# Attention with two expert layers: two state-read buffers, rank sums on TensorE, routing steps side by side

## The chip, the cores and the metric

The kernel runs on one core of one Trainium2 chip. The metric is the time on the device in microseconds, as the median of several runs; lower is better. In the rows PE is TensorE and PEld its weight loads, DVE is VectorE, ACT is ScalarE, POOL is GpSimd, and SP is SyncE, which issues most DMAs.

## What is computed

An attention in both directions between 512 tokens and 32 state slots gives four batches of 544 rows, N = 2176 rows of 512 columns. Two expert layers follow; the first has a capacity per expert, so a row's rank among the rows of its expert matters. The reference, cut:

```python
a  = softmax(scale * x @ state.T);  xread = a  @ state    # x (4, 8, 512, 64), state (4, 8, 32, 64)
a2 = softmax(scale * state @ x.T);  sread = a2 @ x
x  = concat([xread, sread], axis=2).transpose(0, 2, 1, 3).reshape(N, 512)
# layer 1: 8 experts, w1 (8, 512, 1024), w2 (8, 1024, 512); layer 2 the same, without cap
logits = x @ w_gate; expert = argmax(logits); gate = softmax(logits)[expert]
for i in range(N):
    e = expert[i]
    if counts[e] < cap: disp[e, counts[e]] = x[i]; pos[i] = counts[e]; counts[e] += 1; keep[i] = True
y = relu(disp @ w1) @ w2
out[i] = gate[i] * y[expert[i], pos[i]] if keep[i] else 0
```

## The kernel before

**Attention.** `slot(b)` works on batch b: it transposes the softmax of the state side (`e2n`), reads the state for the tokens (`av`) and the tokens for the state (`sr`), and makes scores and softmax of later batches beside it. A slot has seven places, `beside(0)` to `beside(6)`, at which side work runs. The three steps of `sread(b)` stand at places 3, 5 and 6, and those of batches 2 and 3 run on into the next slot or behind the last: `fold` adds the heads on TensorE into a bank `pyT` of PSUM, lets ScalarE copy it to `xs`, and writes `xs` to rows of `xrows` in DRAM; `turn` transposes `xs`; `logits` multiplies it by the gate's weights. The rows of the tokens go to `xrows` from `av`.

**Background work.** Small steps of the routing are generators in one queue, `bgq`. `tick(n)` takes up to n steps of it, `PAUSE` ends a turn, and `abreast` takes steps of several generators in turn. So the order of each engine's instructions is fixed when the program is built, by where `tick` is called: at the places of a slot (99 steps each, from the second slot on) and after each four matmuls (m1) or three (m2) of an expert's product, TQ steps a time. Such a point is called an event.

**Routing.** `route(b0, nb, stops)` handles nb batches: the one-hot of the argmax, the number of earlier rows for the same expert, then `places` (rank, position in the lists) and `gates`, abreast; `stops` are pauses between these parts. It is called for batch 0 alone (`early`), from whose counts `popular` and `load_first` choose and load the first expert's weights, and for batches 1 to 3 in the first expert's product. For the count a VectorE chain adds the rows of a partition (`csb`), two matmuls (`upper`, `ones`) add over the partitions, and VectorE adds batch by batch into `preb`. `plan_runs` then chooses which expert's block runs when; `enlist_all` makes for each batch two one-hots, `loc` and `lov`, and multiplies them on TensorE (list products, five small matmuls a batch) to have lists of rows.

**Expert products.** TensorE runs blocks in the order m1(0), m1(1), m2(0), m1(2), m2(1), ... An m1 block is 12 matmuls into a bank `ph`, an m2 block 12 into four banks `py`. In fp32 each weight and each activation is split in a high part, rounded by a copy to fp32r, and a low part, a subtraction: `xTh`/`xTl`, `hTh`/`hTl`, `w0h`/`w0l` for w1 and `w1h`/`w1l` for w2. ScalarE rounds; VectorE or GpSimd subtracts. `SPLIT0` gives the slot and place at which the four parts of the first w1 are split, `SPLIT2` the events for w2. At the event `PLANNED` the kernel waits (in program order) until the plan is made and asks for the next expert's weights. `fills` writes zeros into `yrows`, the output rows of the first layer, and `fill_out` into `out`, both through SyncE's queue.

Of the kernel before, what the change touches and what calls it, by code (L numbers as in the profile page):

```python
# [74 lines left out]
def moe_kernel(ctx: ExitStack, tc: tile.TileContext, x, state, wg1, w1a, w2a, cap, wg2, w1b, w2b, out):  # L75
# [87 lines left out]
    DVE.memset(wg2q, 0.0)  # L163
    zb = ctile([P, 4 * P], BF16, "zb")
    DVE.memset(zb, 0.0)
# [8 lines left out]
    sums = [ctile([P, P], F32, f"sums{i}") for i in range(2)]  # L174

    zeros = tp.tile([P, ROW], F32, name="zeros")

# [20 lines left out]
    upper = ctile([P, P], BF16, "upper")  # L198
    ones = ctile([P, P], BF16, "ones")
    tidc = ctile([P, B, R + 1], F32, "tidc")  # L200
    tidw = ctile([P, B, R + 1], F32, "tidw")
    smask = ctile([P, B, R + 1], F32, "smask")

    def constants():
        DVE.tensor_scalar(upper, iof[:, 0:P], iop[:, 0:1], None, op0=ALU.is_gt)

        DVE.tensor_scalar(tidc, tid, float(HALF), None, op0=ALU.is_ge)
# [11 lines left out]
        POOL.memset(zeros, 0.0)  # L219
# [53 lines left out]

    def wsplit(which, c, on=ON[2]):
# [376 lines left out]

    def route(b0, nb, stops, early=False):
# [3 lines left out]
        o4, cs, p4 = ohb[:, b0:b0 + nb], csb[:, b0:b0 + nb], preb[:, b0:b0 + nb]  # L656
# [12 lines left out]
        yield from pauses(stops[0])  # L669
        w = nb * 2 * E  # L670
        rsv = rs.rearrange("p b a e -> p (b a e)")
# [3 lines left out]
        prs = pool.tile([P, 2, nb, 2, E], F32, tag="prs", name="prs")  # L675
        DVE.tensor_copy(prs.rearrange("p t b a e -> p (t b a e)"), pyv[:, 0:2 * w])
        yield
        if early:
            yield from popular(rp, 0, prs[:, 1, 0, 0], most)
            yield from load_first(0)  # L680
            yield from pauses(stops[2])
            yield from keep_room(prs[:, 1, 0, 0])
        for i in range(nb):
            for a, r in ((0, 0), (1, R)):
                DVE.tensor_tensor(out=p4[:, i, r], in0=run, in1=prs[:, 0, i, a], op=ALU.add)
                DVE.tensor_tensor(out=run, in0=run, in1=prs[:, 1, i, a], op=ALU.add)
                yield
        yield from pauses(stops[3])
# [11 lines left out]
        def places():  # L700
            DVE.tensor_tensor(out=p4[:, :, 1:R], in0=cs[:, :, 1:R], in1=bc(p4[:, :, 0:1], [P, nb, R - 1, E]), op=ALU.add)
            yield
            far = sel[:, 0, b0 * (R + 1):(b0 + nb) * (R + 1)]
# [13 lines left out]
            DVE.scalar_tensor_tensor(out=flat(ppb, b0, nb), in0=jj, scalar=-float(P), in1=rk, op0=ALU.mult, op1=ALU.add)  # L717
            yield
            if early:
# [4 lines left out]
    lsp = ta.enter_context(tc.tile_pool(name="lists", bufs=2, side="right"))  # L724

    def enlist_all(lag):
# [15 lines left out]
        yield  # L742
        todo = []

# [5 lines left out]
        for b in range(B):  # L750
            oc = lsp.tile([P, R + 1, NT], F16, tag="loc", name="loc")
            ov = lsp.tile([P, R + 1, P], F16, tag="lov", name="lov")
# [4 lines left out]
            DVE.tensor_tensor(out=ov, in0=bc(iof[:, None, 0:P], [P, R + 1, P]), in1=bc(ppb[:, b, :, None], [P, R + 1, P]), op=ALU.is_equal)  # L757
            yield
            if todo:
                product(*todo.pop())  # L760
            todo.append((b, oc, ov))
        yield from pauses(lag)
        product(*todo.pop())
        yield from pauses(1)
# [4 lines left out]
    def when(name, g):  # L769

        while name not in done:
            yield PAUSE
        yield from g

    def fills(*parts):

        g = NTOK // P
        for i in parts:
            lo, hi = g * i // 4, g * (i + 1) // 4
            SP.dma_start(out=yrows.rearrange("(g p) w -> p g w", p=P)[:, lo:hi], in_=bc(zeros[:, None, :], [P, hi - lo, ROW]))  # L780
# [17 lines left out]
    with ExitStack() as ac:  # L798
# [269 lines left out]
        def more(b):  # L1068
            return tuple((i, lambda c=c: wsplit(0, c)) for c, (k, i) in enumerate(SPLIT0) if k == b)
# [574 lines left out]
```

## Time and profile before

| | before |
|---|---|
| median of 3 runs | 473.42 us (472.94 to 473.48) |
| the profiled execution, its own time | 477.82 us |
| its span in the trace | 476.0 us |
| TensorE, busy | 423.3 us, 89% |
| VectorE, ScalarE, GpSimd, busy | 182.5, 165.1, 185.2 us |
| mean granted clock of TensorE | 0.962 of full speed |
| DMA | 88.14 MB, 185 GB/s over the span |

Times in rows belong to the profiled execution, which took 4.4 us more than the median of the runs; its span is what the trace covers, and 1.8 us of its time lie around it. A granted clock of 1.0 is 2.4 GHz, 0.5 the lower level of 1.2 GHz, and the mean of a stretch lies between. Busy shares add up over stages with different limits, so they say only where to look.

### The profile page before, as it was taken

What the parts mean: (1) busy time and instruction counts of PE and PEld (TensorE: products, weight loads), DVE (VectorE), ACT (ScalarE), POOL (GpSimd) and SP (SyncE); (2) the same over time, 40 slices, a digit from 0 to 9 for tenths busy, and PEclk for the clock granted to TensorE, in tenths of its full rate; (3) what the DMA queues carried; (4) which work ended last, traced back from release to release, by engine and by line L of the source; (5) the groups of instructions that cost most, each with busy time, mean ns of one, the idle gap of its engine ahead of it and who ended that gap; (6) DMA issues with size and microseconds to landing.
All of it is one profiled execution on the core that took longest, in us unless ns stands there. A gap on an engine that the chain in (4) does not pass through costs nothing. (4 is left out here: it accounts for less than half of the span.)

```text
span 476.0 us, 7994 instructions
## 1 busy us (share of the span) xinstructions
PE 423.3 (89%) x2726; PEld 305.4 (64%) x2726; DVE 182.5 (38%) x593; ACT 165.1 (35%) x295; POOL 185.2 (39%) x167
## 2 busy tenths in 40 slices
PE   8887389649999899999986899999989999999991
PEld 5665267437865684775764587778745856758771
DVE  6988447973141340141353141981420101411111
ACT  3775365101344411455210345213521213452111
POOL 6441301004414527415443335567543504777003
PEclk9999969959999999999997999999999999999997
DMA  7977932079999975909732200018998958210002
GB/s 234 271 172 205 252 109 51 1 233 164 344 352 389 388 278 184 353 8 361 278 143 86 63 30 1 30 73 292 372 383 254 313 162 304 87 66 23 8 1 88
DMA packets 45990, 88.14 MB, mean 185 GB/s; under 512 B 8528, under 2 KB 19024, under 8 KB 45904
## 3 DMA queue, kind: packets, MB, share of 16 engines
q1 hardware_dynamic: 41104, 72.43, 48.0%
q0 software_dynamic: 4800, 14.71, 8.8%
q8 instruction: 37, 0.61, 0.5%
q14 instruction: 49, 0.40, 0.3%
HBM read 66.65 MB, written 21.52 MB: 185 GB/s over the span
## 5 line engine op out<-in xcount | busy, mean ns | idle before, releaser
L1128 DVE SCALAR_TENSOR_TENSOR hTl<-ph,hTh 128x512 fp32r<-128x512 f32 x48 | 33.2, 691 | 218.2 <-ACT hTh L1127 206.4
L1146 PE MATMUL py<-w1h,hTh 128*128 128x512 f32 x192 | 81.8, 426 | 0.0
L1127 ACT ACTIVATE hTh<-ph 128x512 fp32r<-128x512 f32 x48 | 28.7, 597 | 138.7 <-PE ph L1136 91.3
L1146 PE MATMUL py<-w1h,hTl 128*128 128x512 f32 x192 | 75.6, 394 | 0.0
L1146 PE MATMUL py<-w1l,hTh 128*128 128x512 f32 x192 | 75.5, 393 | 0.0
L1356 POOL TENSOR_TENSOR w0l<-raw,w0h 128x512 fp32r<-128x512 f32 x40 | 50.9, 1288 | 43.5 <-ACT w0h L1355 41.3
L277 POOL TENSOR_TENSOR w1l<-raw,w1h 128x1024 fp32r<-128x1024 f32 x20 | 47.8, 2395 | 43.8 <-ACT w1h L276 43.7
L1136 PE MATMUL ph<-xTh,w0h 128*128 128x512 f32 x192 | 54.6, 406 | 6.4 <-issue 4.0
L1136 PE MATMUL ph<-xTh,w0l 128*128 128x512 f32 x192 | 56.1, 414 | 0.5 <-issue 0.5
L1136 PE MATMUL ph<-xTl,w0h 128*128 128x512 f32 x192 | 56.5, 416 | 0.0
L1136 PEld LDWEIGHTS ph<-xTh,w0h 128*128 128x128 f32 x192 | 35.7, 191 | 15.9 <-issue 5.7
L1136 PEld LDWEIGHTS ph<-xTl,w0h 128*128 128x128 f32 x192 | 35.7, 191 | 13.4 <-issue 6.1
L1146 PEld LDWEIGHTS py<-w1h,hTh 128*128 128x128 f32 x192 | 36.4, 190 | 9.6 <-issue 3.4
L1136 PEld LDWEIGHTS ph<-xTh,w0l 128*128 128x128 f32 x192 | 35.7, 194 | 10.7 <-issue 3.4
L1146 PEld LDWEIGHTS py<-w1h,hTl 128*128 128x128 f32 x192 | 36.3, 189 | 8.2
L1146 PEld LDWEIGHTS py<-w1l,hTh 128*128 128x128 f32 x192 | 36.5, 190 | 6.8 <-issue 1.0
L1164 POOL DMA_INDIRECT out_dram<-ysb,dsti x15 | 14.9, 991 | 61.5 <-ACT ysb L1154 54.0
L1164 POOL DMA_INDIRECT yrows<-ysb,dsti x16 | 16.0, 997 | 29.3 <-DVE oc L335 8.1
L1355 ACT CAST w0h<-raw 128x512 fp32r<-128x512 f32 x40 | 23.8, 617 | 5.8 <-DMA raw<-in_moe_w_dram 3.5
L276 ACT CAST w1h<-raw 128x1024 fp32r<-128x1024 f32 x24 | 25.1, 1046 | 0.0
L950 PE MATMUL pav<-vg,e1T 128*128 128x264 f32 x56 | 16.9, 426 | 3.5 <-ACT lgx L955 3.0
L1295 PE MATMUL pyT<-raw,xTf 128*32 128x256 f32 (+1 forms) x144 | 16.8, 454 | 0.0
(350 smaller groups left out, 555.8 us busy)
## 6 DMA issues: line engine op xcount, KB each, us to landing
raw<-in_moe_w_dram SPq DMA_DIRECT2D x104, 512.0 KB
out_dram<-zb SPq DMA_DIRECT2D x2, 2176.0 KB
yrows<-zeros SPq DMA_DIRECT2D x3, 1026.0 KB
xb<-in_x_dram SPq DMA_DIRECT2D x6, 512.0 KB
xrows<-xr SPq DMA_DIRECT2D x8, 256.0 KB
yrows<-zeros SPq DMA_DIRECT2D x1, 1282.5 KB
xb<-in_x_dram SPq DMA_DIRECT2D x4, 256.0 KB
xrows<-ysb SPq DMA_DIRECT2D x4, 256.0 KB
```

The costliest lines, as they stand in the source:

```text
L276: ACT.copy(h, t)
L277: (POOL if on[c] else DVE).tensor_tensor(out=l, in0=t, in1=h.bitcast(F32), op=ALU.subtract)
L950: PE.matmul(pv[:, a, 0:GW], e1_[b][:, r % 2, a, r // 2], vg[:, b, a], start=True, stop=True)
L1127: ACT.activation(out=hTh[:, c % 2], in_=p, func=AF.Relu)
L1128: DVE.scalar_tensor_tensor(out=hTl[:, c % 2], in0=p, scalar=0.0, in1=hTh[:, c % 2].bitcast(F32), op0=ALU.max, op1=ALU.subtract)
L1136: PE.matmul(p, w[k][:, 0, c * P:(c + 1) * P], u[:, k], start=(i == 0 and k == 0), stop=(i == 2 and k == NC1 - 1))
L1146: PE.matmul(py[t], u[:, c % 2, t * P:(t + 1) * P], w[c // 2][:, c % 2], start=(c == 0 and i == 0), stop=(c == NC2 - 1 and i == 2))
L1164: i = POOL.indirect_dma_start(out=(yrows if L == 0 else out)[:, :], out_offset=bass.IndirectOffsetOnAxis(ap=dsti[:, y:y + 1], axis=0), in_ ...
L1295: PE.matmul(pyv[q * n:(q + 1) * n, 0:w], xTf[:, c, 0:n], w1[c][:, 0, q * w:(q + 1) * w], start=(c == 0), stop=(c == NC1 - 1))
L1355: ACT.copy(h, t)
L1356: (POOL if ON[half][c] else DVE).tensor_tensor(out=l, in0=t, in1=h.bitcast(F32), op=ALU.subtract)
```

## The change

- `xs` becomes two buffers, `xs_[b % 2]`.
- The counts of `route` are added up on TensorE alone: 8 small matmuls in the first call and 16 in the second, with two new constant matrices, `lower` and `identb`, in place of the chain `csb`, two matmuls and the additions batch by batch.
- The places and gates of batch 0 stand later (`stops`), and `drain` behind the last slot.
- In the second call `plan_runs` and the position one-hots `lov` of batches 0 and 1 run abreast with places and gates.
- A list product is placed at least 5 events behind its one-hots; `TQ` is 3 and the event `PLANNED` 20.
- The first weights are all split in the last slot, and VectorE rounds them.
- The tile `zeros` and its memset go; `fills` writes from `zb` in two column parts, 257 and 256 wide.

The diff, cut:

```diff
-SPLIT0 = ((2, 6), (3, 0), (3, 1), (3, 4))
+SPLIT0 = ((3, 0), (3, 1), (3, 2), (3, 4))
-TQ, TQ2, FG, STEP = (5, 2, 1, 3)
-PLANNED, READY, GET = ((14, 29), 36, 0)
+TQ, TQ2, FG, STEP = (3, 2, 1, 3)
+PLANNED, READY, GET = ((20, 29), 36, 0)
...
-        ACT.copy(h, t)
+        if quick:
+            DVE.tensor_copy(h, t)
+        else:
+            ACT.copy(h, t)
...
-    xs = tp.tile([NS, DM], F32, name="xs")
+    xs_ = [tp.tile([NS, DM], F32, name=f"xs{i}") for i in range(2)]
...
-        rs = pool.tile([P, nb, 2, E], BF16, tag="rs2", name="rs")
-        DVE.tensor_copy(rs[:, :, 1], o4[:, :, R])
-        DVE.tensor_copy(cs[:, :, 1], o4[:, :, 0])
-        yield
-        for r in range(2, R):
-            DVE.tensor_tensor(out=cs[:, :, r], in0=cs[:, :, r - 1], in1=o4[:, :, r - 1], op=ALU.add)
-            yield
-        DVE.tensor_tensor(out=rs[:, :, 0], in0=cs[:, :, R - 1], in1=o4[:, :, R - 1], op=ALU.add)
+        rs = pool.tile([P, nb, E], BF16, tag="rs2", name="rs")
+        with nc.allow_low_precision("counts up to four"):
+            DVE.tensor_reduce(out=rs, in_=o4[:, :, 0:R].rearrange("p b r e -> p b e r"), axis=AX.X, op=ALU.add)
...
-        PE.matmul(pyv[:, 0:w], upper, rsv, start=True, stop=True)
-        PE.matmul(pyv[:, w:2 * w], ones, rsv, start=True, stop=True)
+        add(got, upper, bc(rs[:, :, None], [P, nb, c, E]), True)
+        for r in range(R - 1):
+            add(got[:, :, r + 1:R], identb, bc(o4[:, :, r:r + 1], [P, nb, R - 1 - r, E]))
+        add(got[:, :, R], lower, rs)
+        add(got[:, :, R], upper, o4[:, :, R])
+        for b in range(nb - 1):
+            for x in (rs[:, b:b + 1, None], o4[:, b:b + 1, R:R + 1]):
+                add(got[:, b + 1:], ones, bc(x, [P, nb - 1 - b, c, E]))
+        for b in range(nb):
+            add(tot, ones, bc(rs[:, b:b + 1], [P, 2, E]), b == 0)
+        for b in range(nb):
+            add(tot[:, 1], ones, o4[:, b, R])
...
-        yield from abreast(places(), gates())
+        yield from abreast(places(), gates(), *beside_)
...
+            while todo and todo[0][0] <= clock[0]:
+                product(*todo.popleft()[1:])
+            todo.append((clock[0] + lag, b, oc, ov_[b]))
...
-            SP.dma_start(out=yrows.rearrange("(g p) w -> p g w", p=P)[:, lo:hi], in_=bc(zeros[:, None, :], [P, hi - lo, ROW]))
+            for a, w in ((0, ROW - DM // 2), (ROW - DM // 2, DM // 2)):
+                SP.dma_start(out=yrows.rearrange("(g p) w -> p g w", p=P)[:, lo:hi, a:a + w], in_=bc(zb.bitcast(F32)[:, None, 0:w], [P, hi - lo, w]))
...
-        bgq.append(route(0, 1, (2, 0, 1, 3), True))
+        bgq.append(route(0, 1, (2, 0, 5, 7), True))
...
-        drain()
-        slot(3, TICKS[3], steps((0, reads[2][2]), *zip(READ[0:2], reads[3]), *more(3)))
+        drain()
...
-    bgq.append(chain(route(1, B - 1, (4, 1, 0, 0)), plan_runs(rp, 0), fills(2, 3), named("listed", enlist_all(3))))
+    bgq.append(chain(route(1, B - 1, (3, 0, 0, 0), False, (plan_runs(rp, 0), chain(positions(0), until_placed(), positions(1)))), fills(2, 3), named("listed", enlist_all(5))))
```

Three places in the order of the instructions show what this moves. On VectorE, before, around the one-hots of the first list product: `sel` to `ekb` find each row's list slot, then come `loc` and `lov` of the first batch.

```order
L732 TENSOR_TENSOR sel_192<-ohb,abc 128x160 x3
L734 TENSOR_REDUCE sum_1313<-sel_192 128x60
L736 TENSOR_TENSOR ekb<-jjb,sum_1313 128x20
L737 TENSOR_TENSOR sum_1313<-sum_1313,jjb 128x20
L739 TENSOR_TENSOR ekb<-ekb,sum_1313 128x20
L741 TENSOR_TENSOR ekb<-ekb,sum_1313 128x20
L753 TENSOR_TENSOR loc<-iof,ekb 128x260
L755 TENSOR_TENSOR loc<-loc,tidc 128x260
L757 TENSOR_TENSOR lov<-iof,ppb 128x640
```

The same place after:

```order
L755 TENSOR_TENSOR sel_193<-ohb,abc 128x160 x3
L757 TENSOR_REDUCE sum_1317<-sel_193 128x60
L1151 SCALAR_TENSOR_TENSOR hTl<-ph_1077,hTh 128x512
L759 TENSOR_TENSOR ekb<-jjb,sum_1317 128x20
L760 TENSOR_TENSOR sum_1317<-sum_1317,jjb 128x20
L762 TENSOR_TENSOR ekb<-ekb,sum_1317 128x20
L764 TENSOR_TENSOR ekb<-ekb,sum_1317 128x20
L280 TENSOR_TENSOR w1l_1055<-raw_149,w1h_1051 128x1024
L1358 UNCONDITIONAL_BRANCH
L775 TENSOR_TENSOR loc<-iof,ekb 128x260
L1358 UNCONDITIONAL_BRANCH
L777 TENSOR_TENSOR loc<-loc,tidc 128x260
```

The low half of m1's fourth block and the subtraction of a w2 part now stand ahead of the first `loc`, and `lov` of the first batch has moved further up, into the plan. On TensorE, before, the products stand in m1's fourth block (`ph_1074` here), the first two together behind four of its matmuls:

```order
L748 LDWEIGHTS lov
L748 MATMUL listp<-loc,lov 128x52
L1136 MATMUL ph_1074<-xTh,w0l_156 128x512
L1136 MATMUL ph_1074<-xTh,w0l_157 128x512
L1136 MATMUL ph_1074<-xTh,w0l_158 128x512
L1136 MATMUL ph_1074<-xTh,w0l_159 128x512
```

After, the first stands at the end of m2's third block, ahead of m1's fifth (`ph_1076`):

```order
L771 LDWEIGHTS lov
L771 MATMUL listp<-loc,lov 128x52
L1159 MATMUL ph_1076<-xTh,w0h_153 128x512
L1159 MATMUL ph_1076<-xTh,w0h_154 128x512
L1159 MATMUL ph_1076<-xTh,w0h_155 128x512
L1159 MATMUL ph_1076<-xTh,w0h_156 128x512
```

Each list product is ten rows there (five pairs of a weight load and a matmul); the first two no longer stand together, and one product stands behind each four matmuls of m1. On SyncE, before, the next expert's w1 (four loads, the last shown) is asked for ahead of the second part of the fill:

```order
L272 DMA raw_144<-in_moe_w_dram 128x1024
L1335 UNCONDITIONAL_BRANCH x2
L780 DMA yrows<-zeros 128x4x513
L780 DMA yrows<-zeros 128x5x513
L1326 TENSOR_LOAD ri_124
```

After:

```order
L803 DMA yrows<-zb 128x4x257
L803 DMA yrows<-zb 128x4x256
L803 DMA yrows<-zb 128x5x257
L803 DMA yrows<-zb 128x5x256
L1349 TENSOR_LOAD ri_125
L1358 COMPARE_AND_BRANCH
L1349 TENSOR_LOAD ri_125
L272 ISA
L272 DMA raw_142<-in_moe_w_dram 128x1024
```

The fill stands ahead of the weights, in four pieces.

## Rows read from the trace of the kernel before

**Rows 1.** Page, part 1: busy time, share and instructions of each engine.

```profile
PE 423.3 (89%) x2726; PEld 305.4 (64%) x2726; DVE 182.5 (38%) x593; ACT 165.1 (35%) x295; POOL 185.2 (39%) x167
```

**Rows 2.** Windows: us, busy (instructions) of PE, PEld, DVE, ACT, POOL, PEclk, DMA, GB/s.

```profile
54.40:61.00 6.60, 0.01 (x1) 0.01 (x1) 0.00 (x0) 0.64 (x2) 0.30 (x1) 0.71 1.10 121
61.00:67.40 6.40, 6.40 (x28) 5.09 (x28) 3.86 (x5) 5.06 (x10) 0.00 (x0) 0.50 0.23 80
90.90:102.10 11.20, 0.95 (x11) 0.63 (x10) 10.75 (x48) 0.00 (x0) 0.21 (x1) 0.67 0.38 116
102.10:108.30 6.20, 6.20 (x19) 4.57 (x19) 3.34 (x7) 1.53 (x2) 0.00 (x0) 0.50 0.98 260
```

**Rows 3.** Timeline of ScalarE, TensorE: start, us, instruction [idle before <-releaser].

```profile
52.94 0.19 ACT L955 COPY lgx<-pav 128x16 f32<-128x16 f32 x1
...
60.37 0.57 ACT L613 COPY xs<-pyT 32x512 f32<-32x512 f32 x1 [7.24 <-DMA xrows<-xs]
...
60.99 0.63 PE L618 MATMUL pyT<-ident,xs 32*128 32x32 f32 x4 [6.66 <-ACT xs L613]
```

**Rows 4.** Timeline of TensorE at the list products.

```profile
100.16 0.51 PE L748 MATMUL listp<-loc,lov 128*128 128x52 f16 x5 [9.22 <-DVE lov L757]
...
101.69 0.51 PE L748 MATMUL listp<-loc,lov 128*128 128x52 f16 x5 [1.03 <-DVE lov L757]
```

**Rows 5.** Timeline of places and gates of batch 0, first, middle and last.

```profile
44.11 0.14 DVE L701 TENSOR_TENSOR preb<-csb,preb 128x24 f32<-128x24 bf16 x1
...
44.39 0.24 ACT L303 ACTIVATE rd<-rd 128x40 f32<-128x40 f32 x1 [1.78 <-DVE rd L301]
...
46.53 0.17 DVE L397 TENSOR_TENSOR mde<-mde,tid 128x4 f32<-128x4 f32 x1
```

**Rows 6.** Timeline of the last slot's end, up to the first m1 block.

```profile
61.62 1.30 DVE L931 STREAM_TRANSPOSE e1T<-u 128x512 f32<-128x512 f32 x2
...
74.69 2.48 DVE L1111 TENSOR_TENSOR xTl<-py,xTh 128x512 fp32r<-128x512 f32 x4
...
75.74 1.17 PE L1136 MATMUL ph<-xTh,w0h 128*128 128x512 f32 x4 [0.79 <-issue]
```

**Rows 7.** Timeline of VectorE in the plan and the list one-hots.

```profile
90.64 0.22 DVE L485 TENSOR_TENSOR pah<-key 128x64 f32<-128x64 f32 x1
...
93.34 1.22 DVE L277 TENSOR_TENSOR w1l<-raw,w1h 128x1024 fp32r<-128x1024 f32 x1
...
97.83 0.18 DVE L736 TENSOR_TENSOR ekb<-jjb,sum 128x20 f32<-128x20 f32 x1
...
98.94 0.43 DVE L755 TENSOR_TENSOR loc<-loc,tidc 128x260 f16<-128x260 f16 x1
...
99.28 0.82 DVE L757 TENSOR_TENSOR lov<-iof,ppb 128x640 f16<-128x640 f32 x1
...
114.18 0.69 DVE L1128 SCALAR_TENSOR_TENSOR hTl<-ph,hTh 128x512 fp32r<-128x512 f32 x1 [3.50 <-ACT hTh L1127]
```

**Rows 8.** View of line L834: count, ns least/mean/most, first to last start.

```profile
L834 DVE COPY dup<-st x2: 428/632/836, 4.1 to 4.4; 128x512 f32<-128x512 f32 x2
```

**Rows 9.** Timeline of TensorE in m1's fifth block.

```profile
110.55 1.09 PE L1136 MATMUL ph<-xTh,w0h 128*128 128x512 f32 x4
...
113.35 0.39 PE L1146 MATMUL py<-w1h,hTh 128*128 128x512 f32 x1
```

**Rows 10.** Timeline of TensorE at the rank sums.

```profile
82.11 0.20 PE L672 MATMUL pyT<-rs,upper 128*128 128x48 bf16 x1
```

**Rows 11.** Windows, the same columns: the fill of `out` and the second fill of `yrows`.

```profile
142.00:150.00 8.00, 8.00 (x39) 3.62 (x36) 0.77 (x2) 2.58 (x5) 2.17 (x2) 1.00 1.09 387
106.00:118.00 12.00, 12.00 (x52) 9.47 (x51) 3.77 (x11) 2.13 (x3) 5.27 (x5) 0.90 1.06 163
```

**Rows 12.** Timeline of the next expert's w1: asked for, first rounded.

```profile
97.15 2.06 SPq L272 DMA_DIRECT2D raw<-in_moe_w_dram  x4
...
119.63 0.61 ACT L1355 CAST w0h<-raw 128x512 fp32r<-128x512 f32 x1
```

More of the change, by code (lines that the diff above doesn't have):

```diff
@@ L163, in moe_kernel @@
     DVE.memset(wg2q, 0.0)
-    zb = ctile([P, 4 * P], BF16, "zb")
+    zb = ctile([P, 4 * P + 2], BF16, "zb")
     DVE.memset(zb, 0.0)
@@ L174, in moe_kernel @@
     sums = [ctile([P, P], F32, f"sums{i}") for i in range(2)]
-    zeros = tp.tile([P, ROW], F32, name="zeros")
     def iota(t, pattern, base, cm):
@@ L199, in moe_kernel @@
     ones = ctile([P, P], BF16, "ones")
+    lower = ctile([P, P], BF16, "lower")
+    identb = ctile([P, P], BF16, "identb")
     tidc = ctile([P, B, R + 1], F32, "tidc")
@@ L205, in constants @@
         DVE.tensor_scalar(upper, iof[:, 0:P], iop[:, 0:1], None, op0=ALU.is_gt)
+        DVE.tensor_scalar(lower, iof[:, 0:P], iop[:, 0:1], None, op0=ALU.is_le)
+        DVE.tensor_copy(identb, ident)
         DVE.tensor_scalar(tidc, tid, float(HALF), None, op0=ALU.is_ge)
@@ L217, in constants @@
         DVE.tensor_reduce(out=jp, in_=m4, axis=AX.X, op=ALU.add)
-        POOL.memset(zeros, 0.0)
         n = SMALL[0]
@@ L272, in wload, with wsplit @@
             SP.dma_start(out=t, in_=src[:, c * k:(c + 1) * k, :])
-    def wsplit(which, c, on=ON[2]):
+    def wsplit(which, c, on=ON[2], quick=False):
         t, h, l = raw[0][which][c], wset[which][0][c], wset[which][1][c]
-        ACT.copy(h, t)
+        if quick:
+            DVE.tensor_copy(h, t)
+        else:
+            ACT.copy(h, t)
         (POOL if on[c] else DVE).tensor_tensor(out=l, in0=t, in1=h.bitcast(F32), op=ALU.subtract)
@@ L608, in sread @@
     def sread(b):
+        xs = xs_[b % 2]
         def fold():
@@ L650, in flat, with route @@
         return t.rearrange("p b r e -> p (b r) e") if len(t.shape) == 4 else t.rearrange("p b r -> p (b r)")
[L652 removed]
+    def route(b0, nb, stops, early=False, beside_=()):
         n, run, pool = nb * (R + 1), runs_[0], Tagged(b0)
         lg, gt, oh, pre = flat(lgs, b0, nb), flat(gts, b0, nb), flat(ohb, b0, nb), flat(preb, b0, nb)
[L656 removed]
+        o4 = ohb[:, b0:b0 + nb]
         mv = []
@@ L668, in route @@
+        with nc.allow_low_precision("counts up to four"):
+            DVE.tensor_reduce(out=rs, in_=o4[:, :, 0:R].rearrange("p b r e -> p b e r"), axis=AX.X, op=ALU.add)
         yield
         yield from pauses(stops[0])
-        w = nb * 2 * E
-        rsv = rs.rearrange("p b a e -> p (b a e)")
-        PE.matmul(pyv[:, 0:w], upper, rsv, start=True, stop=True)
-        PE.matmul(pyv[:, w:2 * w], ones, rsv, start=True, stop=True)
+        c = R + 1
+        w = n * E
+        got = pyv[:, 0:w].rearrange("p (b r e) -> p b r e", b=nb, r=c)
@@ new lines, in route, with add @@
+        tot = pyv[:, w:w + 2 * E].rearrange("p (a e) -> p a e", a=2)
+        def add(out, m, x, start=False):
+            PE.matmul(out, m, x, start=start, stop=True, skip_group_check=not start)
+        add(got, upper, bc(rs[:, :, None], [P, nb, c, E]), True)
[6 more added lines that the diff above has]
+                add(got[:, b + 1:], ones, bc(x, [P, nb - 1 - b, c, E]))
@@ L674, in route @@
+        for b in range(nb):
+            add(tot, ones, bc(rs[:, b:b + 1], [P, 2, E]), b == 0)
+        for b in range(nb):
+            add(tot[:, 1], ones, o4[:, b, R])
         yield from pauses(stops[1])
-        prs = pool.tile([P, 2, nb, 2, E], F32, tag="prs", name="prs")
-        DVE.tensor_copy(prs.rearrange("p t b a e -> p (t b a e)"), pyv[:, 0:2 * w])
-        yield
         if early:
-            yield from popular(rp, 0, prs[:, 1, 0, 0], most)
+            kept = pool.tile([P, w + 2 * E], F32, tag="kept", name="kept")
+            DVE.tensor_copy(kept, pyv[:, 0:w + 2 * E])
+            got = kept[:, 0:w].rearrange("p (b r e) -> p b r e", b=nb, r=c)
+            tot = kept[:, w:w + 2 * E].rearrange("p (a e) -> p a e", a=2)
+            yield
+            yield from popular(rp, 0, tot[:, 0], most)
@@ L680, in route @@
             yield from load_first(0)
             yield from pauses(stops[2])
[L682 to L687, printed above, removed]
+            yield from keep_room(tot[:, 0])
+        DVE.tensor_tensor(out=pre, in0=got.rearrange("p b r e -> p (b r) e"), in1=bc(run[:, None, :], [P, n, E]), op=ALU.add)
@@ L688, in route @@
+        DVE.tensor_tensor(out=run, in0=tot[:, 1], in1=run, op=ALU.add)
+        yield
         yield from pauses(stops[3])
@@ L700, in places @@
         def places():
-            DVE.tensor_tensor(out=p4[:, :, 1:R], in0=cs[:, :, 1:R], in1=bc(p4[:, :, 0:1], [P, nb, R - 1, E]), op=ALU.add)
-            yield
             far = sel[:, 0, b0 * (R + 1):(b0 + nb) * (R + 1)]
@@ L718, in places, with positions @@
             yield
+            done.add(f"placed{b0}")
             if early:
                 yield from take(v[:, 0:R], rk[:, 0:R], jj[:, 0:R])
-        yield from abreast(places(), gates())
+        yield from abreast(places(), gates(), *beside_)
     lsp = ta.enter_context(tc.tile_pool(name="lists", bufs=2, side="right"))
+    ov_ = {}
+    def positions(*bs):
+        for b in bs:
+            ov_[b] = ov = lsp.tile([P, R + 1, P], F16, tag="lov", name="lov")
+            DVE.tensor_tensor(out=ov, in0=bc(iof[:, None, 0:P], [P, R + 1, P]), in1=bc(ppb[:, b, :, None], [P, R + 1, P]), op=ALU.is_equal)
+            yield
     def enlist_all(lag):
@@ L742, in enlist_all @@
         yield
-        todo = []
+        todo = deque()
         def product(b, oc, ov):
@@ L756, in enlist_all @@
             yield
[L757 to L764, printed above, removed]
+            if b > 1:
+                yield from positions(b)
+            while todo and todo[0][0] <= clock[0]:
+                product(*todo.popleft()[1:])
+            todo.append((clock[0] + lag, b, oc, ov_[b]))
+        while todo:
+            while todo[0][0] > clock[0]:
+                yield PAUSE
+            product(*todo.popleft()[1:])
+        yield from pauses(2)
         sv = rtp.tile([P, NT], F32, name="sv0")
@@ L767, in enlist_all, with until_placed @@
         yield from list_out(rows[0], md[0], placed, sv, u)
-    def when(name, g):
-        while name not in done:
+    def until_placed():
+        while "placed1" not in done:
             yield PAUSE
-        yield from g
     def fills(*parts):
@@ L1068, in more @@
         def more(b):
-            return tuple((i, lambda c=c: wsplit(0, c)) for c, (k, i) in enumerate(SPLIT0) if k == b)
+            return tuple((i, lambda c=c: wsplit(0, c, quick=True)) for c, (k, i) in enumerate(SPLIT0) if k == b)
         slot(0, TICKS[0], steps(*zip(READ, reads[0]), (0, lambda: run_all(fills(0, 1)))))
-        bgq.append(route(0, 1, (2, 0, 1, 3), True))
+        bgq.append(route(0, 1, (2, 0, 5, 7), True))
         slot(1, TICKS[1], steps(*zip(READ, reads[1])))
         slot(2, TICKS[2], steps(*zip(READ[0:2], reads[2]), *more(2)))
+        slot(3, TICKS[3], steps((0, reads[2][2]), *zip(READ[0:2], reads[3]), *more(3)))
         drain()
-        slot(3, TICKS[3], steps((0, reads[2][2]), *zip(READ[0:2], reads[3]), *more(3)))
     walloc(ctx.enter_context(tc.tile_pool(name="w2", bufs=1)), 1)
```

6 lines of the change are left out of this document (2 added, 4 removed).

## Prediction

> **What bounds the kernel now.** I read the page first, then the timeline of TensorE's idle stretches, then the engines that ended them. TensorE is busy for 89% of the span [rows 1], so a change can only win where it stands. Two stretches hold most of what is left, and the windows around them show a second price: the granted clock [rows 2].
>
> The first is in the last part of the attention. TensorE is idle from 54.40 to 61.00 with a mean granted clock of 0.71. The next 6.4 us run at 0.50, the lower level of 1.2 GHz, although TensorE is busy in all of them. The reason is one buffer [rows 3]: ScalarE has finished its last copy at 53.13 (52.94 + 0.19), and its next, of pyT into `xs`, starts 7.24 us later, when the DMA that writes the previous `xs` to `xrows` has landed. TensorE's transposes of `xs` wait for that copy, and everything behind them in TensorE's order waits too.
>
> The second is in the first expert's products. The list products of L748 stand 9.22 us and then 1.03 us for VectorE's one-hots, 10.25 us together [rows 4]. In 90.90 to 102.10 VectorE is busy for 10.75 of 11.20 us: it is behind, not idle. The clock is 0.67 over that stretch and 0.50 over the next 6.2 us, all busy, which costs about 3.1 us of TensorE's work [rows 2].
>
> **The change, part by part.** I make the sum against the profiled execution, 477.82 us (476.0 of span and 1.8 around it), and carry the gain over to the median of the three runs, 473.42 us, 4.4 below it.
>
> *Two `xs` buffers.* The copy at 60.37 waits for a write of two slots ago instead of the last one. That write was issued before the weights' eight loads, so I count the whole 7.24 us as gone: **7.2**. The work behind it must then not find another wait; that is the next two items.
>
> *The first rank's places moved behind a slot.* Before, 19 VectorE instructions of places and gates run from 44.11 to 46.70, 2.6 us, ahead of the next softmax's transposes, and ScalarE stands 1.78 us for the first of them before it can go on with e2n [rows 5]. After, they stand in the last slot. Bounds: 0 (something else is as late) to 2.6 us; I take ScalarE's own wait, **1.8**.
>
> *VectorE rounds the first weights, in the last slot.* ScalarE loses four casts there, VectorE gains them, and VectorE is what is late there. Before, VectorE's stream from the end of the last transposes (61.62 + 1.30 = 62.92) to the end of xTl (74.69 + 2.48) is 14.25 us, and m1 begins at 75.74 [rows 6]. After, the same stretch holds the 2.6 us of places, four pairs of cast and subtraction, 0.5 us of two small instructions and the 2.48 us of xTl. The subtraction takes 1.22 us [rows 7]. No row has the cast on VectorE. The nearest is a copy of 512 fp32 elements inside SBUF: 428 ns in one instruction and 836 in the other [rows 8]. The quicker one, with 512 further elements at its own rate (0.428 less some 0.16 us that the smallest instructions take, so 0.27 us), gives 0.70 us; the bound above is the subtraction's 1.22. I take 0.70, since GpSimd is idle in this stretch (POOL 0.00) [rows 2] and the slower copy fell in the start, where all engines work. So 2.6 + 4 x 1.92 + 0.5 + 2.48 = 13.3 us, and with 1 us of waiting for TensorE's last reads 14.3: as long as before, so **0**. With 1.22 it is 2.1 us worse. The half clock of 61.00 to 67.40 I count at nothing here, since VectorE's stream sets the end.
>
> The Trainium skill has a rule for this choice (VectorE: DVE Perf Modes, "Mode 2×_2P — use both read ports for one tensor"): a copy with one source, in SBUF on both sides, runs at two elements a cycle even in fp32, which a subtraction of two tensors can't. The quicker of the two copies of L834 agrees with it, the slower does not. By the rule this term is 0; by the subtraction's 1.22 it is -2.1 and the sum 11.1 in place of 13.2.
>
> *The list wait.* After, VectorE's order between hTl of m1's third block and the first one-hot pair that a product needs is fixed, and so is TensorE's: three blocks of twelve matmuls, 2.8 us each (110.55 to 113.35) [rows 9], so 8.4 us, and then the first list product. VectorE meanwhile has [rows 7]: the handover and hTl (114.18 + 0.69 - 113.35 = 1.52), the plan with its rounding of the weights and the sums (90.64 to 97.83 = 7.19), one position one-hot that now stands inside it (0.82), the next hTl (0.69), the slots and the first pair of rank one-hots (97.83 to 98.94 + 0.43 = 1.54) and a subtraction that now comes first (1.22): 12.98 us. So TensorE still waits, but 12.98 - 8.4 = 4.6 us in place of 10.25: **5.6** less. The later products find their one-hots ready: a pair and a position one-hot are some 1.7 us, and TensorE has 0.9 us of matmuls and 0.5 us of products between them, so they wait little or not at all.
>
> *TensorE adds up the ranks.* The second call issues 16 small matmuls where two were. One takes 0.20 us [rows 10] and they overlap; five list products, of the same kind, take 0.51 us [rows 4], so 14 x 0.10: **-1.4**, on TensorE's path. The first call adds six, 0.6 us, beside VectorE's shorter sum (five small instructions become one), and I count both at 0.
>
> *The clock.* It fell in both waits, of 6.60 and 9.22 us [rows 2, 4], and stood at the lower level for the 6.4 and 6.2 us behind them. The wait that is left, 4.6 us, is shorter than both, so no row decides whether the clock falls in it; it is nearer to 6.6 than to the busy stretches, and I expect the fall and the same half clock for some 6 us behind it: **0** saved, 3.1 if it stays up.
>
> *The fills.* `yrows` is now filled from `zb` in eight DMAs of half rows. The second half of them moves ahead of the next expert's weights in SyncE's order. The fill ran at 163 GB/s (106 to 118), fill_out with its 1024-byte pieces at 387 [rows 11]; so 9 of 17 groups of 128 rows, 2.36 MB, take between 6 and 14.5 us. The weights were asked for at 97.15 and first used at 119.63 [rows 12], 22.5 us, of which the change leaves some 16 (the wait and moving the request from event 14 to event 20 take the rest). The fills are asked for about 6 us ahead of them. With 14.5 us of fill the first of four weight loads has landed with 3 us to spare: **0**. The other edits (memset of zeros gone, `lower` and `identb` built at the start) lie beside loads and cost nothing that I can see; uncovered they are below 0.7 us each way.
>
> Sum: 7.2 + 1.8 + 0 + 5.6 - 1.4 + 0 = 13.2 us; 477.8 - 13.2 = 464.6 profiled, 473.4 - 13.2 = **460.2 us**. What follows the first stage is TensorE's own work, so I carry the whole gain to the end.
>
> **Rivals.**
> 1. The list wait goes altogether, because VectorE's interleaved chains overlap better than my durations say, and the clock stays up: 4.6 and 3.1 more, 20.9, so 452.5 us. For it: small instructions in the plan overlap when they don't depend on each other. Against: hTl stands in VectorE's order and waits for TensorE, and the plan is queued behind it.
> 2. VectorE is the bound in both places: casts at 1.22 (-2.1), nothing from the earlier slot (-1.8), and a list wait of 8 us (-3.4): 5.9, so 467.5 us. For it: VectorE was 96% busy in 90.90 to 102.10. Writes of `xr` and `xb`, queued beside that of `xs`, being the next late thing would look the same in time, up to the same price.
> 3. Slower. The fills take the weights' place in SyncE's queue. If half rows take as long each as whole rows took, the second fill lasts 29 us; the first weights then land about 11 us late, of which TensorE's queued blocks cover 4. From 35 us on, 2.4 times the 14.5, the whole gain is gone; at three times, 43.5 us, the time would be 482 us. Against: the 1024-byte pieces of fill_out ran at 387 GB/s [rows 11], more than twice the rate of the whole rows.
> 4. The change does not do what it says, as a wait on another write of the same slot replaces that on `xs` in full, and the list wait comes back with it: 473 us.
>
> **How the numbers follow.** Chances: forecast 0.50 (its own range 456.5 to 464), rival 1 0.20, rival 2 0.21, rival 3 0.05, rival 4 0.04. The range for 8 in 10 takes in rivals 1 and 2 nearly whole: 452 to 468. About 0.2%, 1 us, is what a measurement of this kernel can tell from no change. Faster by more than that: the forecast and rivals 1 and 2, and a mild rival 3, 0.92; within it 0.03; slower 0.05.
>
> **What the new profile would show.** ScalarE's copy into `xs` starts right behind lgx, and TensorE has no gap over 2 us in the last slot. First matmul of m1 (now L1159) at about 66 to 68 us instead of 75.74. VectorE's cast of `w0h` at 0.6 to 0.8 us. A single wait of L771 for `loc` of 3 to 6 us, with the clock falling in it, and no further wait above 0.5 us at the other three products. The second fill landed before ScalarE needs the next expert's `w0h`. The prediction is wrong if the wait at L771 is absent or above 7 us, if ScalarE stands for `raw` after the first stage, or if m1 starts later than 71 us.

## The result and the profile after

The changed kernel takes 456.86 us (median of 4 runs, 454.92 to 459.18) where the kernel before takes 473.18 us beside it: a ratio of 0.9659, with a 95% interval of 0.9612 to 0.9706. That is 16.3 us less, where 13.2 were forecast. A second comparison (run e5 below) gave 458.52 us against 472.94, 0.9691 with 0.9652 to 0.973: 14.4 us. The time lies inside the range of the prediction (452 to 468), and 456.86 just inside the forecast's own 456.5 to 464.

The first part of the page after, busy time of each engine, answers to [rows 1]:

```profile
PE 421.7 (92%) x2746; PEld 304.0 (66%) x2746; DVE 182.8 (40%) x576; ACT 161.3 (35%) x291; POOL 184.9 (40%) x166
```

TensorE works 1.6 us less than before in a span that is 18.6 us shorter (457.4 for 476.0): nearly all that went is time in which it stood. Some 2.3 of the 18.6 us belong to the choice of executions, since the two profiled ones lie 4.6 and 2.3 us above the medians of their kernels. Where the time went is read best from the start of the same block in both traces. Three such blocks of m1 are the sixth of the first expert, the first of the second layer, and one near the end. In the brackets stands the idle time before an instruction and what ended it; `issue` means that the timeline names nothing for it, PEq is TensorE's sequencer. First the timeline of TensorE before:

```profile
116.10 1.09 PE L1136 MATMUL ph<-xTh,w0h 128*128 128x512 f32 x4
...
254.25 2.06 PE L1136 MATMUL ph<-xTh,w0h 128*128 128x512 f32 x4 [3.23 <-issue]
...
451.61 1.17 PE L1136 MATMUL ph<-xTh,w0h 128*128 128x512 f32 x4 [0.71 <-PEq L1549]
```

and the same blocks after, with the first m1 of all, which stood at 75.74 [rows 6], ahead of them:

```profile
66.66 1.17 PE L1159 MATMUL ph<-xTh,w0h 128*128 128x512 f32 x4 [1.05 <-POOL ysb L1610]
...
102.13 1.10 PE L1159 MATMUL ph<-xTh,w0h 128*128 128x512 f32 x4
...
236.87 2.07 PE L1159 MATMUL ph<-xTh,w0h 128*128 128x512 f32 x4 [0.40 <-issue]
...
433.71 1.17 PE L1159 MATMUL ph<-xTh,w0h 128*128 128x512 f32 x4 [0.71 <-PEq L1572]
```

The lead is 9.08 us at the first m1, 13.97 behind the lists, 17.38 at the start of the second layer and 17.90 near the end. The first two are the places that the prediction speaks of (9.0 and 13.2 there); the 3.4 us at the second layer are in no term of it.

The timeline of ScalarE, TensorE and VectorE in the last slots after shows the copy into `xs` without a wait, where it stood 7.24 us [rows 3], and the casts on VectorE, between the end of the transposes `e1T` and `xTl`:

```profile
49.13 0.57 ACT L618 COPY xs<-pyT 32x512 f32<-32x512 f32 x1
...
51.36 1.29 DVE L954 STREAM_TRANSPOSE e1T<-u 128x512 f32<-128x512 f32 x2
...
52.58 0.64 DVE L277 CAST w0h<-raw 128x1024 fp32r<-128x1024 f32 x1
53.26 1.22 DVE L280 TENSOR_TENSOR w0l<-raw,w0h 128x1024 fp32r<-128x1024 f32 x1
...
54.73 0.24 ACT L306 ACTIVATE rd<-rd 128x40 f32<-128x40 f32 x1 [2.10 <-DVE rd L304]
...
58.92 1.62 PE L617 MATMUL pyT<-ysr,ident 128*32 128x128 f32 x8 [1.75 <-DVE ysr L990]
...
65.24 2.48 DVE L1134 TENSOR_TENSOR xTl<-py,xTh 128x512 fp32r<-128x512 f32 x4
```

ScalarE's wait for the gates of batch 0 has not gone: it stands at 54.73 with 2.10 us, where it was 1.78 [rows 5]. TensorE's longest wait of the slot, 1.75 us, is for `ysr` of VectorE (the read of the tokens for the state, scaled), behind the casts and the places. At the lists, the timeline and the windows of the wait and of what follows it (columns as in [rows 2]) answer to [rows 4] and to the lower rows of [rows 2]:

```profile
90.94 0.49 PE L771 MATMUL listp<-loc,lov 128*128 128x52 f16 x5 [4.08 <-DVE loc L777]
...
93.23 0.55 PE L771 MATMUL listp<-loc,lov 128*128 128x52 f16 x5
```
```profile
86.86:90.94 4.08, 0.01 (x2) 0.00 (x1) 3.98 (x12) 0.00 (x0) 0.00 (x0) 0.88 1.08 239
90.94:100.10 9.16, 9.16 (x36) 6.24 (x36) 5.06 (x13) 0.60 (x1) 0.00 (x0) 0.50 1.12 217
```

One wait of 4.08 us in place of 10.25, none at the next product, and the half clock behind it for 9.16 us of work.

### The profile page after: what moved, and what is told of

Read it like the earlier page. It is cut to its first block, busy times and chain, and to the rows that moved or that the text cites. A ratio compares the mean times of both kernels' runs of the same rounds, so it can differ in the third digit from the quotient of the medians.

```text
span 457.4 us, 8003 instructions
## 1 busy us (share of the span) xinstructions
PE 421.7 (92%) x2746; PEld 304.0 (66%) x2746; DVE 182.8 (40%) x576; ACT 161.3 (35%) x291; POOL 184.9 (40%) x166
```

## The experiments

Each stands beside runs of the kernel before. Edits are against the changed kernel unless it says otherwise, and are cut to the lines that matter.

**e1: two buffers alone, on the kernel before.** The second buffer takes the room of `zeros`, so the fills from `zb` come with it, at their old place in the queue.

```diff
...
-    xs = tp.tile([NS, DM], F32, name="xs")
+    xs_ = [tp.tile([NS, DM], F32, name=f"xs{i}") for i in range(2)]
...
```

> The kernel before with two buffers of state reads alone (and the fills from zb in two column parts, which make the room for the second buffer; their place in the queue is that of before). Theory of the prediction: the wait of 7.24 us at the copy into xs goes and nothing takes its place, m1 begins 6 to 8 us earlier than 75.74, the list wait stays about 10 us, and the time is 465 to 468 us. Rival: another wait of the last slot (VectorE's stream, or the writes of xr) takes the place of most of it, m1 begins less than 4 us earlier and the time is above 469 us.

467.12 us against 473.05, ratio 0.987 (0.9848 to 0.9892): 5.9 us less. TensorE's timeline:

```profile
69.78 0.47 PE L1137 MATMUL ph<-xTh,w0h 128*128 128x512 f32 x1 [0.80 <-issue]
...
94.16 0.51 PE L748 MATMUL listp<-loc,lov 128*128 128x52 f16 x5 [9.18 <-DVE lov L757]
...
247.62 0.78 PE L1137 MATMUL ph<-xTh,w0h 128*128 128x512 f32 x1 [3.14 <-issue]
```

m1 begins 5.96 us earlier than 75.74, and the waits at the lists and at the second layer stay. The theory holds: the time is inside its range, m1's lead just under its 6 to 8 us.

**e2: one buffer again.**

```diff
-    xs_ = [tp.tile([NS, DM], F32, name=f"xs{i}") for i in range(2)]
+    xs_ = [tp.tile([NS, DM], F32, name="xs")] * 2
```

> The changed kernel with one buffer of state reads again. Theory: the copy into xs waits again for a write that is queued behind the first expert's weights, TensorE stands about 7 us in the slots 2 and 3 and the time is 463 to 466 us. Rival: in the new order VectorE sets the end of the slot anyway and most of the wait is hidden: under 460 us.

462.96 us, 0.9792 (0.9774 to 0.9809). The timeline of ScalarE and TensorE:

```profile
58.38 0.57 ACT L618 COPY xs<-pyT 32x512 f32<-32x512 f32 x1 [9.04 <-DMA xrows<-xs]
```
```profile
59.01 0.63 PE L623 MATMUL pyT<-ident,xs 32*128 32x32 f32 x4 [8.46 <-ACT xs L618]
...
73.53 0.70 PE L1159 MATMUL ph<-xTh,w0h 128*128 128x512 f32 x2 [0.65 <-issue]
```

The wait is back, m1 is 6.87 us later than 66.66, and the time 4.4 to 6.1 us above the two medians of the changed kernel: the theory, at 462.96 us just under its range.

**e3: ScalarE rounds the first weights.**

```diff
-            return tuple((i, lambda c=c: wsplit(0, c, quick=True)) for c, (k, i) in enumerate(SPLIT0) if k == b)
+            return tuple((i, lambda c=c: wsplit(0, c)) for c, (k, i) in enumerate(SPLIT0) if k == b)
```

> The changed kernel with ScalarE rounding the first weights, in the same places. Theory: VectorE's stream sets the end of the last slot, so taking 2.7 us of casts (4 x 0.67) from it brings m1 forward by 1 to 2.5 us from 66.66, 454 to 456 us. Rival: ScalarE's copies in the slot stand behind the four casts of about 1.04 us, m1 begins 1 to 4 us later, 458 to 461 us. The prediction's own number for the choice was 0.

457.88 us, 0.9695 (0.9667 to 0.9723): between the two medians of the changed kernel, so neither theory's size is there. m1 begins at 65.81, 0.3 to 0.9 us earlier, and TensorE now waits 2.09 us for ScalarE's cast in the slot where it waited 1.75 for `ysr`:

```profile
57.68 1.16 PE L973 MATMUL psT<-vg,e1T 128*128 128x264 f32 x4 [2.09 <-ACT w0h L279]
```

The prediction's 0 for the choice holds, as far as these runs can tell.

**e4: list products later.**

```diff
-    bgq.append(chain(..., named("listed", enlist_all(5))))
+    bgq.append(chain(..., named("listed", enlist_all(16))))
```

> The changed kernel with each list product placed 16 counts behind its one-hots in place of 5 (the first in the middle of m2's fourth block, some 4.2 us of matmuls later). Theory: TensorE no longer waits 4.08 us, and without the wait its clock stays at the upper level where it was at half from about 90 to 100 us, worth another 4 to 4.6 us: 448 to 450 us. Rival 1: the clock falls for another reason, so only the wait is saved: 452.5 to 453.5 us. Rival 2: the lists are late for the next block's gather, and the wait comes back there: no faster than 455 us.

451.76 us, 0.9555 (0.9541 to 0.957). The window from the start of m1's fourth block to that of its sixth, and the first two products in the timeline:

```profile
81.47:93.89 12.42, 12.42 (x65) 9.48 (x63) 12.11 (x47) 2.14 (x3) 0.21 (x1) 1.00 0.97 176
```
```profile
91.21 0.39 PE L771 MATMUL listp<-loc,lov 128*128 128x52 f16 x5
92.33 0.40 PE L771 MATMUL listp<-loc,lov 128*128 128x52 f16 x5
```

TensorE is busy all through at a granted clock of 1.00, while VectorE is as busy as ever (12.11 of 12.42). Wait and half clock are both gone, as the theory has it; the time is 5.1 to 6.8 us under the changed kernel's, short of its 448 to 450 and past the 452.5 to 453.5 of rival 1. The runs lie within 1.1 us (451.35 to 452.43), where those of the changed kernel spread over 4 to 5.

**e5: the changed kernel once more.**

> The changed kernel once more, beside the three that follow. Theory: the gain is that of the first stage of its trace, 13.9 us at the end of the first expert (75.74 to 66.66 at m1's start, the rest at the lists), so the median lies at 457 to 460 us; its runs spread by some 4 us because TensorE's clock falls in some executions and not in others at the start of the second layer. Rival: the 3.4 us more that the trace shows at the start of the second layer (254.25 to 236.87) are part of it in every run: 455 to 456.5 us.

458.52 us (455.41 to 459.90). Of the ten runs of both comparisons five lie at 458.5 to 459.9 us and five at 454.9 to 457.2. The profiled execution here took 455.41 us, the first one 459.18, and the windows at the lists tell them apart:

```profile
86.37:90.42 4.05, 0.00 (x0) 0.00 (x0) 3.95 (x12) 0.00 (x0) 0.00 (x0) 0.74 1.10 236
90.42:95.20 4.78, 4.78 (x21) 3.11 (x21) 3.82 (x8) 0.00 (x0) 0.00 (x0) 0.50 1.09 181
95.20:100.00 4.80, 4.80 (x29) 3.71 (x29) 1.84 (x9) 0.60 (x1) 0.84 (x1) 1.00 1.06 362
```

The wait is the same, 4.05 for 4.08 us, but the lower clock stands for 4.78 us of work behind it in place of 9.16, which is 2.2 us of time. The start of the second layer, where the theory looked for the fall of the clock, does not tell them apart: it is 0.50 there in both, for 3.33 us from 236.87 in the first execution and for 3.10 us from 235.10 in this one. The ten times go with the mean granted clock of their executions, 0.966 to 0.976 in the five slower and 0.981 to 0.987 in the five faster ones; where it fell in those without a trace is not known. Of the 3.4 us at the second layer the medians settle nothing between the two theories: 458.52 is the first one's, 456.86 nearer the rival's.

**e6: plan, one-hots and products as before,** one behind the other (`TQ` 5, `PLANNED` 14, `enlist_all` of before, the weights ahead of the fill).

```diff
...
-    bgq.append(chain(route(1, B - 1, (3, 0, 0, 0), False, (plan_runs(rp, 0), chain(positions(0), until_placed(), positions(1)))), fills(2, 3), named("listed", enlist_all(5))))
+    bgq.append(chain(route(1, B - 1, (4, 1, 0, 0)), plan_runs(rp, 0), fills(2, 3), named("listed", enlist_all(3))))
```

> The changed kernel with plan, one-hots and list products in the order of before (one behind the other, five steps an event, the weights asked for ahead of the second fill). Theory: the list wait is about 10 us again in place of 4.08, the clock is lost in both, so it is 5 to 6 us slower than the changed kernel, 462 to 463.5 us. Rival: the half clock that follows the short wait in the changed kernel costs as much as the longer wait does, and the difference is under 3 us.

460.80 us, 0.9744 (0.9707 to 0.9782): 2.3 us above the changed kernel beside it (3.9 above its first median), with overlapping intervals: nearer the rival's size. The windows of the wait and behind it:

```profile
80.40:88.70 8.30, 0.02 (x1) 0.02 (x2) 8.09 (x36) 0.00 (x0) 0.21 (x1) 0.62 0.94 193
88.70:92.60 3.90, 3.90 (x17) 2.65 (x17) 3.80 (x9) 0.00 (x0) 0.00 (x0) 0.50 1.14 162
```

The wait is 8.30 us (not 10.25; likely because the ranks on TensorE leave VectorE less ahead of the lists, which no run shows alone), and the clock is back after 3.90 us of work. The wait is 4.2 us longer, and 0.4 to 2.6 us of time come back in the half clock.

**e7: ranks added up as before** (`csb`, two matmuls, sums batch by batch).

```diff
-        rs = pool.tile([P, nb, E], BF16, tag="rs2", name="rs")
...
-        for b in range(nb):
-            add(tot[:, 1], ones, o4[:, b, R])
...
+        PE.matmul(pyv[:, 0:w], upper, rsv, start=True, stop=True)
+        PE.matmul(pyv[:, w:2 * w], ones, rsv, start=True, stop=True)
```

> The changed kernel with the ranks added up as before (VectorE's chain, two matmuls, sums batch by batch). Theory: the 16 small matmuls cost TensorE 0.48 us, not the 1.9 of the prediction, and the ten small VectorE instructions that come back stand ahead of the list one-hots, so the list wait grows by 1 to 2 us from 4.08 and the time by 0.5 to 1.5 us. Rival, the prediction's term: TensorE's matmuls are the dearer side, and the time falls by 1 us or more.

462.62 us, 0.9781 (0.9739 to 0.9823): 4.1 us slower than the changed kernel, more than either theory gave. TensorE's timeline:

```profile
67.15 1.17 PE L1147 MATMUL ph<-xTh,w0h 128*128 128x512 f32 x4 [0.65 <-issue]
...
92.94 0.39 PE L759 MATMUL listp<-loc,lov 128*128 128x52 f16 x5 [2.53 <-DVE loc L765]
...
238.03 1.21 PE L1147 MATMUL ph<-xTh,w0h 128*128 128x512 f32 x2 [2.89 <-issue]
```

The list wait did not grow: more steps in the background put the products later too, and it fell to 2.53 us. Of what is lost the trace places 2.5 us at the second layer, 2.89 us for 0.40; m1 also begins 0.5 to 1.0 us later. What makes the rest is open.

**e8: places of batch 0 ahead of the last slot.**

```diff
-        bgq.append(route(0, 1, (2, 0, 5, 7), True))
+        bgq.append(route(0, 1, (2, 0, 1, 3), True))
...
+        drain()
         slot(3, TICKS[3], steps((0, reads[2][2]), *zip(READ[0:2], reads[3]), *more(3)))
-        drain()
```

> The changed kernel with the places and gates of batch 0 ahead of the last slot as before. Theory, the prediction's term: ScalarE stands about 1.8 us for the gates again ahead of e2n, and m1 begins 1 to 2.6 us later than 66.66, 458 to 460 us. Rival: VectorE's stream through the last slot is as long in either order and TensorE's wait for ysr (1.75 us) gets shorter for it, so that m1 begins within 0.7 us of 66.66 and the time stays.

456.21 us, 0.9641 (0.9595 to 0.9687), 2.3 us under the changed kernel beside it, with overlapping intervals. ScalarE stands 1.44 us for the gates, its next copy into `xs` comes 2.7 us later than in the changed kernel (51.85 for 49.13), and yet m1 begins earlier, in the timeline of ScalarE and TensorE:

```profile
51.85 0.57 ACT L618 COPY xs<-pyT 32x512 f32<-32x512 f32 x1
...
59.27 1.06 PE L617 MATMUL pyT<-ysr,ident 128*32 128x128 f32 x8 [0.26 <-DVE ysr L990]
...
65.36 0.94 PE L1159 MATMUL ph<-xTh,w0h 128*128 128x512 f32 x3 [0.94 <-POOL ysb L1610]
```

65.36 for 66.66 and 66.16: the rival, and in this execution past it. `ysr` costs 0.26 us instead of 1.75. e10 below has the same first stage and begins m1 at 66.40.

**e9: the kernel before with 20 small matmuls more in its warm-up.**

```diff
         warm(WARM)
+        for _ in range(20):
+            PE.matmul(pyv[:, 0:8], zb[:, 0:P], zb[:, 0:8], start=True, stop=True)
```

> The kernel before with 20 further matmuls of 8 columns in its warm-up, so many as the change adds for the ranks, and nothing else. In every trace with the short code of TensorE (before, two buffers alone, ranks on VectorE) TensorE stands 2.9 to 3.2 us at the start of the second layer for nothing that the profile shows; in the six with 20 matmuls more ahead of it, 0.4 us. Theory: it is the place of TensorE's code that decides, so the wait falls to about 0.4 us here too and the time to 469.5 to 471.5 us. Rival: the wait hangs on what the first stage leaves behind (the list order, the times of GpSimd's work), so it stays at about 3 us and the time at 472.5 to 474 us.

472.27 us, 0.9977 (0.995 to 1.0004), 1.2 us less and not clear of none, and just under the rival's range. The trace is clear, in TensorE's timeline:

```profile
58.49 0.63 PE L618 MATMUL pyT<-ident,xs 32*128 32x32 f32 x4 [4.17 <-ACT xs L613]
...
248.21 1.21 PE L1138 MATMUL ph<-xTh,w0h 128*128 128x512 f32 x2 [0.40 <-issue]
```

The wait at the second layer falls to 0.40 us; in every kernel with the longer code it is 0.40 to 0.46. The timeline names nothing for it, but the view of the branch just ahead of the block does (count, ns, start; PEldq is TensorE's sequencer at its weight loads), before from 250.9 to 254.3 us and in e9 from 247 to 248.3:

```profile
L1424 PEldq COMPARE_BRANCH  x1: 3014/3014/3014, 251.1 to 251.1; - x1
```
```profile
L1426 PEldq COMPARE_BRANCH  x1: 328/328/328, 247.7 to 247.7; - x1
```

The same branch takes 2.89 to 3.09 us in the three other traces with the short code (e1, e7, e12) and 0.32 to 0.33 us in the nine others with the long one. In the DMA view a transfer of the instruction queue q8 falls inside the wait in each of the four traces with the long branch, and none falls into the 4 us ahead of the block in the ten with the short one. Before, from 251.02 to 254.25 us (count, MB, share):

```profile
q8 instruction: 1, 0.02, 2.4%
```

So the wait is the branch's, and in fourteen traces it goes with the length of the code ahead of it, whatever the times of the first stage; e9 changed nothing else.

**e12: the kernel before, profiled again** (474.1 us).

> A second profile of the kernel before. Theory: the two waits of the first stage (about 7 and 10 us) and the one of about 3 us at the start of the second layer stand in it again, so they are no accident of one execution. Rival: the wait at the start of the second layer is under 1 us here and was chance.

```profile
59.80 0.42 PE L618 MATMUL pyT<-ident,xs 32*128 32x32 f32 x2 [5.17 <-ACT xs L613]
...
98.64 0.51 PE L748 MATMUL listp<-loc,lov 128*128 128x52 f16 x5 [9.20 <-DVE lov L757]
...
252.39 1.21 PE L1136 MATMUL ph<-xTh,w0h 128*128 128x512 f32 x2 [3.10 <-issue]
```

TensorE's timeline has all three waits again. The one for `xs` is 5.17 us here and 4.17 in e9, where [rows 3] have 6.66: its size changes with the execution.

**e10 and e11: the two findings together.** e10 has the edits of e4 and e8, e11 that of e3 besides.

> The changed kernel with list products 16 counts behind their one-hots and with the places of batch 0 ahead of the last slot as before. Theory: the two gains are in different stages and add up: m1 begins at 65 to 65.8 us, TensorE has no wait at the lists, 449.5 to 451 us. Rival: with m1 earlier the next expert's weights or rows are late and the second gain is lost, 451.5 to 453 us.

> The kernel of the run before this one, with ScalarE rounding the first weights. Theory: with the places gone from the last slot VectorE has room, so that the choice is worth less than 0.7 us either way. Rival: VectorE is still what the end of the slot waits for, and the time falls by 1 us or more.

e10: 449.81 us, 0.951 (0.9473 to 0.9547); e11: 451.28 us, 0.9539 (0.9492 to 0.9585). e10 beats both kernels: 23.7 us under the one before, 7.1 to 8.7 under the changed one, and 2 us under e4, with intervals that just overlap. The theory's time holds, but not its size for the first stage: m1 begins at 66.40, behind the 65 to 65.8 that it gave.

```profile
66.40 1.17 PE L1159 MATMUL ph<-xTh,w0h 128*128 128x512 f32 x4 [0.65 <-issue]
```

From 50 to 58 us the mean granted clock is 0.79 here and 1.00 in e8. e11 is 1.5 us above e10, with overlapping intervals: whose casts they are makes no difference that these runs can tell.

## Why the prediction was right, and where it was not

**Two buffers: right, mis-sized.** The prediction took the whole 7.24 us of one execution. Alone it was worth 5.9 us, and taking it back cost 4.4 to 6.1. The wait hangs on when a write lands that was issued behind eight weight loads (at 46.31, the loads from 38.51 on), and three executions of the same order had 6.66, 5.17 and 4.17 us. The profiled one was the dearest.

**Places behind a slot: not there.** The step that failed is "I take ScalarE's own wait, 1.8": the wait was moved, not removed (2.10 us at 54.73). The earlier slot does gain, as the copies into `xs` at 49.13 and, in e8, 51.85 show. But in the last slot the same instructions stand ahead of `ysr` on VectorE, TensorE waits 1.75 us for that, and the gain is lost again by m1. With the places late m1 begins between 66.16 and 66.91 in four executions (the changed kernel twice, e4, e6), with them early at 65.36 (e8) and 66.40 (e10). So they gained nothing. Whether they cost something is not settled: e8 is 2.3 us faster than e5 and e10 2 us faster than e4, with overlapping intervals both times. The last slot was not "as long as before" either: VectorE's stream from the end of `e1T` to that of `xTl` takes 15.07 us (52.65 to 67.72) for the 14.25 of before, and m1 stands 14.01 us behind `e1T` for 12.82. That m1 began where the forecast has it, at 66.66, is in part luck: errors of opposite sign.

**VectorE's casts: right.** 0.64 to 0.69 us each for the 0.70 that was taken, and no difference in e3. VectorE's stream alone does not set the end of the slot, though, as the prediction took it: at m1 the profile names GpSimd's clearing of `ysb`, 1.05 us, and 1.92 in e5. By the Trainium skill's rule (VectorE: DVE Perf Modes, "Mode 2×_2P — use both read ports for one tensor") a one-source copy inside SBUF runs at two elements a cycle; the trace agrees, with 0.64 us beside 1.22 for the subtraction of as many elements.

**The list wait: right.** 4.6 us forecast, 4.08 and 4.05 measured, and no wait at the later products. e4 shows that it was the order that made TensorE wait and not a want of time on VectorE: with the products a block and a half later nothing waits.

**The clock: right that it falls, mis-sized behind it.** "Some 6 us" were 9.16 in one execution and 4.78 in another, 4.6 or 2.4 us of time. This fits the spread of the runs, the 2.3 us that e6's longer wait cost, and the gain of e4 beyond the 4.05 us of its wait; two executions with a trace are too few to put a size on each.

**The ranks: wrong.** "14 x 0.10" is too dear: the 16 matmuls stand between 72.34 and 72.82, in 0.48 us, since they overlap more closely than the list products.

```profile
72.34 0.23 PE L675 MATMUL pyT<-rs,upper 128*128 128x120 bf16 x1
...
72.82 0.47 PE L1169 MATMUL py<-w1h,hTh 128*128 128x512 f32 x1
```

And the edit gained where a loss was forecast: e7 without it is 4.1 us slower. But 2.5 us of that stand in e7's trace at the branch ahead of the second layer, in no term of the prediction, and go with the place of the code (e9). What the sums on TensorE give by themselves is not shown.

**The fills: right.** SyncE's timeline after, with ScalarE's first cast of the next expert's weights:

```profile
82.02 3.65 SPq L803 DMA_DIRECT2D yrows<-zb  x4
88.54 2.06 SPq L272 DMA_DIRECT2D raw<-in_moe_w_dram  x4
```
```profile
105.67 0.61 ACT L1378 CAST w0h<-raw 128x512 fp32r<-128x512 f32 x1
```

The cast names no wait: it runs behind `hTh` at once, with the fills ahead of the weights. Rival 3 did not come. ScalarE does stand for `raw` later, 5.7 us in three waits from 309 us on, which the prediction took for a sign of being wrong; the kernel before stands so too, 3.5 us in two waits from 326, and TensorE's lead stays (17.38 and 17.90).

**The sum.** The 13.2 us of the prediction stand beside 13.97 in the trace behind the lists, with the misses on `xs`, places and ranks partly cancelling: that it comes so close is in part luck. The single parts, taken one at a time (5.9 for `xs`, 2.3 for the lists, 4.1 for the ranks, -2.3 for the places, 0 for the casts), make 10.0 and not 14.4: they share waits and the half clock, and some are known to 2 us only.

**What stays open.** In profiled executions the place of TensorE's code decides 2.5 to 2.8 us at the second layer: the kernel before, e1, e7 and e12 have 2.89 to 3.23 us, e9 with only the warm-up longer 0.40. How much of this a run without the profiler pays is not settled: e9's time fell by 1.2 us with an interval that reaches no change, e7's rose by 4.1. The padding costs some time of its own, which was not measured apart.

## What to carry to other kernels

A buffer that is written out through a queue with large loads ahead of it wants a second copy, and such a wait should be sized from two profiles. Where one engine waits for a chain on another that is busy but has slack later, move the consumer back by blocks: here it removed the wait and the half clock behind it, and its 5.1 to 6.8 us are more than the 2.3 to 3.9 that taking back the reordering of the chain cost. A wait that the timeline puts down to nothing may stand in the rows of a branch. A wait on an engine's row is worth its length only if what is late next waits for that engine.

## What the runs showed of the hardware

- Behind the same wait of about 4.05 us the granted clock stayed at 0.50 for 9.16 us in one execution and 4.78 in another.
- A branch of TensorE took 3.01 us (before), and 0.33 us (e9) with 20 matmuls more in the warm-up as the only difference; the first block behind it waited 3.23 and 0.40 us. The Trainium skill (Runtime: NRT & Kernel Launch, "Instruction fetch mechanics") says that a taken branch to code outside the part held on chip must wait for a fetch. The rows agree: an instruction transfer on q8 falls inside the wait in all four traces that have it, and in none of the ten others. No view says which engine that queue serves, or whether the branch was taken.
- A VectorE instruction of four columns took as long as a subtraction of GpSimd beside it. In the timeline before, at the start of the second layer:

```profile
251.45 2.42 DVE L409 TENSOR_TENSOR els<-els,elu 128x4 f32<-128x4 f32 x1
251.47 2.37 POOL L277 TENSOR_TENSOR w1l<-raw,w1h 128x1024 fp32r<-128x1024 f32 x1
```

In the changed kernel the same instruction takes 0.16 us (236.90), ahead of GpSimd's subtraction; the next one takes 3.10 us and ends with it (240.19 and 240.16).
